# Softplus and split ahead of the weight conversion in each slot, and the sums of weight blocks on VectorE instead of GpSimd, in a decayed attention plus softplus FFN kernel

## The chip, the cores and the metric

The kernel runs on one core of a Trainium2 chip. The metric is the device time of one execution in microseconds (us); three timed runs before the change gave 600.14, 600.64 and 601.68 us, median 600.64. A core has five engines that each work through their own list of instructions in order and wait for each other by semaphores: TensorE (PE, with its weight loads shown as PEld), VectorE (DVE), ScalarE (ACT), GpSimd (POOL) and SyncE (SP, which issues most DMAs).

## What is computed

A causal attention without softmax, with a decay per head, over 4 sequences, 8 heads, 768 positions and 64 channels; its output, as 3072 tokens of width 512, goes through a feed-forward layer of width 2048 with a softplus between its two products.

```
for b in range(nb):
    intra = einsum('bhic,bhjc->bhij', qb, kb) * Dmask[None]
    intra = einsum('bhij,bhjd->bhid', intra, vb)
    inter = einsum('bhid,bhde->bhie', qb * lam_pow[None], kv_state)
    out[:, :, sl] = intra + inter
    kv_state = lam_block * kv_state + einsum('bhsd,bhse->bhde', kb_dec, vb)
h = x @ w_in
g = maximum(h, 0.0) + log1p(exp(-abs(h)))
return g @ w_out
```

## The kernel before

Tokens are worked on in six chunks of 512 (`NCH`), the feed-forward width in 16 blocks of 128 (`NF`). Each 32-bit product is made of three matmuls on operands split into a high and a low part: ACT writes the high part (a cast), DVE the low part (a subtraction from the high one). So what PE consumes always comes from an ACT step followed by a DVE step.

Every order is written out by hand: each engine runs its instructions in the order in which the program's lines emit them.

**Chunks 0 and 1.** The loop over `s` from 4 to 31 (line 657) is made of slots. Slot s holds the first product of chunk s // 16 with block s % 16 (`mlp1`, L421, 12 matmuls into a bank `h`) and, some slots later, the second product for an earlier slot (`mlp2`, L442, 12 matmuls). In between stand the softplus of the slot before (`chain_act`, ACT L402, from bank `h` to `l`), its split (`chain_hi`, ACT L406, and `chain_lo`, DVE L410, into tile `g`), and in slots 4 to 15 the conversion of the weights, which arrive as raw 64-bit numbers. A group of two weight blocks, tile `c`, is begun in one slot by ACT (`w_scale` L217, `w_round` L221) and DVE (`w_shift` L225, `w_sign` L229, `w_add` L235), and finished in the next slot by ACT (`w_hi` L238) and DVE (`w_lo` L242), which write tile `w`. In an even slot, the group that is finished there is the one that this slot's `mlp1` reads.

Attention comes in units of one pair of heads and one chunk. In slots 6, 9, 12 and 15 `scores_of` puts the score products on PE and, behind `w_add`, the masking (L338) and four state updates (L343) on DVE. In slots 5, 8, 11 and 14 the unit's output product `z` (L326 and L330) follows, with `x_high` (ACT L375) and `x_low` (DVE L393). From slot 16 on, every even slot runs `event`, which does the output of one unit and the scores of the next; its first instructions on PE are the `z` products of unit 8, which need the state updates of slot 15. `k_decay` (ACT L289, tile `kd`) and `q_decay` (DVE L296, `qd`) stand at the top of the slot before a unit's scores; in slot 15 they belong to unit 9, whose input `att` is loaded by SP (L86) into a buffer that the `z` products of slot 14 set free.

**Sums of weight blocks.** Chunks 2 to 5 need fewer first products, at the price of sums of weight blocks: seven products `P1` to `P7` (L588) on combinations of blocks. `block_sums(i)` (L514) forms the sums for one pair of weight blocks in tiles `full` and `sums` on POOL: two additions of 512 columns and four of 256. `store_sums` (L528) splits them (ACT L531, DVE L532) into a tile `parts`, and `send_sums` sends that to DRAM, from where `load_w1` fetches it later. All this is done in slots 16 to 31, one pair per two slots.

**Chunk 2's entry.** In slots 29 to 31 and right behind them the combinations of x are formed: `x_sums_early` and `x_sums_late` (DVE L568 to L577) and `x_block` (ACT L560, DVE L561, tiles `xcP1` to `xcP7`). Then the loop over i from 0 to 7 (line 735) runs, for each pair of weight blocks, P1 into bank `a`, P6 into `b`, P5 into `c`, then P2, P7, P4, P3. ACT copies `a` to `p1` (L753) behind P1, and P2, which adds to the same bank, has to wait for this copy.

```
        old, new = w_group(s - 1), w_group(s)
        if old:
            w_hi(*old)
        chain_act(s - 1)
        chain_hi(s - 1)
        if old:
            w_lo(*old)
        chain_lo(s - 1)
```

## Time and profile before

| what | before |
|---|---|
| median of three runs | 600.64 us |
| the profiled execution, its own time | 599.66 us |
| its span, first to last instruction | 597.7 us |
| PE busy | 578.1 us, 97% of the span |
| DVE busy | 309.6 us, 52% |
| ACT busy | 256.6 us, 43% |
| POOL busy | 53.3 us, 9% |
| L518, additions of 512 columns on POOL | 16, mean 1461 ns |
| L523 to L526, of 256 columns on POOL | 32, means 790 to 858 ns |

The profile's page gives busy times by engine and by 40 slices, the chain of work that ended last, and the costliest groups of instructions. The answers of the trace used below are: busy time in chosen stretches (windows), who waited for whom (waits), and the instructions in order of time (timeline). A row of the timeline has the start, the length, the engine, the line, the operation, what is written and read, the count, and in brackets how long the engine sat idle before it and what ended that. A busy PE is not PE at its peak, since matmuls are pipelined and their ends are modelled. PE is busy nearly all the time, so what counts is where it isn't.

### The profile page before, as it was taken

How to read it: one execution, taken by the hardware profiler on the slowest of the kernel's cores; microseconds unless marked ns; L12 is line 12 of the kernel's file. 1: busy time of each engine (PE TensorE's matmuls, PEld its weight loads, DVE VectorE, ACT ScalarE, POOL GpSimd, SP SyncE). 2: the span in 40 equal slices, each digit the busy share in tenths (PEclk: the TensorE clock that was granted, in tenths of full speed). 3: DMA queues.
4: the chain of work that ended last, by engine and by line, in shares of the span. 5: the costliest groups of instructions: out<-in, count | busy, mean ns of one | idle time of the engine just before them, and what ended most of it. 6: DMA issues, size and time to landing. Idle time of an engine off the chain costs nothing.

```text
span 597.7 us, 12023 instructions
## 1 busy us (share of the span) xinstructions
PE 578.1 (97%) x5203; PEld 471.9 (79%) x5203; DVE 309.6 (52%) x444; ACT 256.6 (43%) x416; POOL 53.3 (9%) x59
## 2 busy tenths in 40 slices
PE   8899898979999999999999999999999999999997
PEld 6676776758888888888888888888888888888886
DVE  7778988886556537735433443285133333333410
ACT  3776677653444436453432423463142222224310
POOL 2000000063533440000000000000000000000000
PEclk9999899998999999999999999999999999999999
DMA  8996546884599996889635556489357453474101
GB/s 293 406 407 252 178 153 197 276 268 165 186 389 393 408 416 256 328 312 394 226 135 194 198 207 234 173 296 362 133 212 316 145 196 136 145 268 141 62 1 70
DMA packets 38452, 142.34 MB, mean 238 GB/s; under 512 B 3712, under 2 KB 5760, under 8 KB 31360
## 3 DMA queue, kind: packets, MB, share of 16 engines
q1 hardware_dynamic: 35808, 136.86, 62.7%
q10 hardware_dynamic: 2592, 4.72, 2.1%
q8 instruction: 41, 0.67, 0.4%
q14 instruction: 11, 0.09, 0.0%
HBM read 112.20 MB, written 29.36 MB: 237 GB/s over the span
## 4 chain that ended last, share of the span: by engine, by line
PE 81%; DMA 11%; DVE 5%; ACT 1%; issue 1%; SPq 1%; DVEq 0%
PE o L607 31%; PE b L588 11%; PE h L421 9%; PE o L442 9%; PE a L588 7%; PE c L588 7%; DMA raw<-in_wts 6%; DMA g<-w 2%; PE z L326 2%; DMA att<-in_att 2%; PE x L311 2%; PE z L330 1%; DVE c L229 1%; DVE c L235 1%; DVE st L343 1%
## 5 line engine op out<-in xcount | busy, mean ns | idle before, releaser
L607 PE MATMUL o<-w,g 128*128 128x512 f32 x816 | 192.7, 390 | 0.0
L607 PEld LDWEIGHTS o<-w,g 128*128 128x128 f32 x816 | 152.5, 188 | 31.9
L421 PE MATMUL h<-x,w 128*128 128x512 f32 x384 | 96.0, 400 | 3.1 <-DVE w L242 2.8
L421 PEld LDWEIGHTS h<-x,w 128*128 128x128 f32 x384 | 72.1, 191 | 21.5 <-DVE w L242 4.5
L442 PE MATMUL o<-w,g 128*128 128x512 f32 x336 | 82.4, 394 | 1.1 <-DVE w L242 0.8
L442 PEld LDWEIGHTS o<-w,g 128*128 128x128 f32 x336 | 62.4, 188 | 15.2 <-DVE w L242 1.1
L588 PE MATMUL a<-xcP,w1a 128*128 128x512 f32 x192 | 48.8, 389 | 0.0
L588 PE MATMUL b<-xcP,w1b 128*128 128x512 f32 x192 | 48.7, 389 | 0.0
L755 DVE TENSOR_TENSOR ta<-b,ta 128x512 f32<-128x512 f32 x16 | 11.1, 691 | 62.9 <-PE b L588 62.9
L588 PEld LDWEIGHTS a<-xcP,w1a 128*128 128x128 f32 x192 | 36.0, 188 | 7.6
L588 PEld LDWEIGHTS b<-xcP,w1b 128*128 128x128 f32 x192 | 36.0, 188 | 7.5
L410 DVE TENSOR_TENSOR g<-l,g 128x512 fp32r<-128x512 f32 x32 | 24.8, 774 | 28.6 <-ACT g L406 28.6
L599 DVE TENSOR_TENSOR g<-lb,g 128x512 fp32r<-128x512 f32 x32 | 21.1, 688 | 34.1 <-ACT g L595 34.1
L763 DVE TENSOR_TENSOR tb<-b,ta 128x512 f32<-128x512 f32 x16 | 11.1, 691 | 52.7 <-PE b L588 52.7
L402 ACT ACTIVATE l<-h 128x512 f32<-128x512 f32 x32 | 19.0, 594 | 35.2 <-PE h L421 32.2
L518 POOL TENSOR_TENSOR full<-w 128x512 f32<-128x512 f32 x16 | 23.0, 1461 | 123.0 <-PE o L442 122.6
L760 ACT ACTIVATE la<-a 128x512 f32<-128x512 f32 x16 | 9.6, 598 | 54.6 <-PE a L588 54.6
L338 DVE TENSOR_TENSOR a<-x,mask 128x512 f32<-128x512 f32 x15 | 10.4, 692 | 41.4 <-PE x L311 21.5
L753 ACT COPY ta<-a 128x512 f32<-128x512 f32 x16 | 9.4, 586 | 52.1 <-PE a L588 52.1
L238 ACT CAST w<-c 128x1024 fp32r<-128x1024 f32 (+1 forms) x19 | 17.4, 913 | 29.2 <-DVE c L235 29.2
L326 PEld LDWEIGHTS z<-qd,st 64*64 64x64 f32 x640 | 17.6, 138 | 11.6 <-issue 11.2
L595 ACT CAST g<-lb 128x512 fp32r<-128x512 f32 x32 | 18.8, 619 | 18.4 <-PE o L607 17.6
(100 smaller groups left out, 803.4 us busy)
## 6 DMA issues: line engine op xcount, KB each, us to landing
w<-g SPq DMA_DIRECT2D x39, 1024.0 KB, 5.0
att<-in_att SPq DMA_DIRECT2D x48, 512.0 KB, 8.6
raw<-in_wts SPq DMA_DIRECT2D x32, 512.0 KB, 10.2
w1a<-g SPq DMA_DIRECT2D x16, 1024.0 KB, 6.4
g<-w SPq DMA_DIRECT2D x24, 512.0 KB, 8.8
w1b<-g SPq DMA_DIRECT2D x16, 768.0 KB, 6.2
g<-parts SPq DMA_DIRECT2D x16, 512.0 KB, 10.3
out_dram<-ob ACTq DMA_DIRECT2D x18, 256.0 KB, 2.2
```

Of the source, the lines that this page charges most:

```text
L238: nc.scalar.copy(out=w_at(ks)[:, 0], in_=conv[ks[0]].bitcast(F32))
L311: nc.tensor.matmul(x[r, cols], lhsT=k[r, b, t], rhs=q[r, b, t], start=True, stop=True)
L326: nc.tensor.matmul(w[half(t), s, cols], lhsT=st[r, b, t], rhs=qd[r, b, t], start=True, stop=False)
L402: nc.scalar.activation(l_tiles[s], h_tiles.pop(s), AF.Softplus)
L410: nc.vector.tensor_sub(out=g[:, 1, :], in0=l_tiles.pop(s), in1=g[:, 0, :])
L421: nc.tensor.matmul(h_tiles[s], lhsT=w[:, i, cs], rhs=x[:, j, :], start=p == 0 and n == 0, stop=p == NP - 1 and n == 2,)
L442: nc.tensor.matmul(o_tiles[c][b], lhsT=g[:, i, b * 128 : (b + 1) * 128], rhs=w[:, j], start=f == 0 and n == 0, stop=f == NF - 1 and n == 2,)
L518: nc.gpsimd.tensor_add(out=full[:, n], in0=w[:, 0], in1=w[:, 1])
L588: nc.tensor.matmul(to, lhsT=w[:, k, n, p * 128 : (p + 1) * 128], rhs=x[:, j, p], start=start and p == 0 and m == 0, stop=p == 1 and m == 2 ...
L595: nc.scalar.copy(out=g[:, 0], in_=l)
L599: nc.vector.tensor_sub(out=g[:, 1], in0=l, in1=g[:, 0])
L607: nc.tensor.matmul(outs[c, b], lhsT=g[:, i, b * 128 : (b + 1) * 128], rhs=w[:, j], start=f == 0 and n == 0, stop=f == NF - 1 and n == 2,)
```

## The change

Two things change. In each slot of chunks 0 and 1, the softplus of the slot before and both halves of its split are emitted ahead of the finishing of the weights; and the finishing's DVE half (`w_lo`) stays ahead of the new group's DVE steps, but behind `w_scale` and `w_round` in the program's text, which are on ACT. Second, the sums of weight blocks go from POOL to DVE. They are formed two slots later (pair 0 in slot 18 instead of 16, and so on), stored two slots later and sent two slots later, and the last pair is formed, stored and sent at the beginning of i = 1 of chunk 2's loop.

```diff
-            nc.gpsimd.tensor_add(out=full[:, n], in0=w[:, 0], in1=w[:, 1])
+            nc.vector.tensor_add(out=full[:, n], in0=w[:, 0], in1=w[:, 1])
...
-        nc.gpsimd.tensor_add(out=s1, in0=a21, in1=a22)
-        nc.gpsimd.tensor_sub(out=s3, in0=a11, in1=a21)
-        nc.gpsimd.tensor_sub(out=s2, in0=s1, in1=a11)
-        nc.gpsimd.tensor_sub(out=s4, in0=a12, in1=s2)
+        nc.vector.tensor_add(out=s1, in0=a21, in1=a22)
+        nc.vector.tensor_sub(out=s3, in0=a11, in1=a21)
+        nc.vector.tensor_sub(out=s2, in0=s1, in1=a11)
+        nc.vector.tensor_sub(out=s4, in0=a12, in1=s2)
...
+        chain_act(s - 1)
+        chain_hi(s - 1)
+        chain_lo(s - 1)
         old, new = w_group(s - 1), w_group(s)
         if old:
             w_hi(*old)
-        chain_act(s - 1)
-        chain_hi(s - 1)
-        if old:
-            w_lo(*old)
-        chain_lo(s - 1)
         if new:
             w_scale(*new)
             w_round(*new)
+        if old:
+            w_lo(*old)
...
-        if s > NF + 1 and s % 2 == 0:
-            send_sums((s - NF) // 2 - 1)
+        if s > NF + 2 and s % 2 == 0:
+            send_sums((s - NF) // 2 - 2)
...
-        if s >= NF and s % 2 == 0:
-            block_sums((s - NF) // 2)
-        if s >= NF and s % 2:
-            store_sums((s - NF) // 2)
+        if s > NF and s % 2 == 0:
+            block_sums((s - NF) // 2 - 1)
+        if s > NF + 2 and s % 2:
+            store_sums((s - NF - 1) // 2 - 1)
...
-    send_sums(NF // 2 - 1)
     chain_act(last - 1)
     chain_hi(last - 1)
     chain_lo(last - 1)
+    send_sums(NF // 2 - 2)
     x_sums_late(2, 1)
...
         for i in range(NF // 2):
+            if more and i == 1:
+                block_sums(NF // 2 - 1)
+                store_sums(NF // 2 - 1)
+                send_sums(NF // 2 - 1)
```

On ACT, at the top of slot 10, before the change (`c18` is the weight group that is finished, `c20` the one that is begun, `h9` the first product of slot 9):

```order
L238 CAST w9_1068<-c18_992 128x1024
L402 ACTIVATE l9_1070<-h9_1050 128x512
L406 CAST g9_1072<-l9_1070 128x512
L217 ACTIVATE c20_1076<-raw20_897 128x1024
L221 ACTIVATE raw20_897<-raw20_897 128x1024
```

And with the change:

```order
L402 ACTIVATE l9_1068<-h9_1050 128x512
L406 CAST g9_1070<-l9_1068 128x512
L238 CAST w9_1073<-c18_991 128x1024
L217 ACTIVATE c20_1075<-raw20_897 128x1024
L221 ACTIVATE raw20_897<-raw20_897 128x1024
```

The softplus and the split of `h9` now stand ahead of the cast of the weights, and `w_scale` directly behind that cast. On DVE, in slots 8 and 9, before the change:

```order
L235 ISA c16_913<-raw16_770,c16_913 128x2048
L393 TENSOR_TENSOR x_1_0_754<-z5_931,x_1_0_754 128x2x4x64
L242 TENSOR_TENSOR w8_984<-c16_913,w8_984 128x1024
L410 TENSOR_TENSOR g8_988<-l8_986,g8_988 128x512
L225 TENSOR_SCALAR c18_992<-c18_992 128x1024
```

And with the change:

```order
L235 ISA c16_912<-raw16_770,c16_912 128x2048
L393 TENSOR_TENSOR x_1_0_754<-z5_931,x_1_0_754 128x2x4x64
L410 TENSOR_TENSOR g8_986<-l8_984,g8_986 128x512
L242 TENSOR_TENSOR w8_989<-c16_912,w8_989 128x1024
L225 TENSOR_SCALAR c18_991<-c18_991 128x1024
```

The low part of the split (L410) and the finishing of the weights (L242) have changed places. On DVE at the beginning of i = 1 of chunk 2's loop (`g2_1` is the split of i = 0, `b2_1` the bank of P6), before the change:

```order
L599 TENSOR_TENSOR g2_1_2959<-tb2_0_2901,g2_1_2959 128x512
L296 TENSOR_TENSOR qd_18_3087<-att18_2787,lp_127 128x512
L755 TENSOR_TENSOR ta2_1_3089<-b2_1_3092,ta2_1_3089 128x512
```

And with the change:

```order
L599 TENSOR_TENSOR g2_1_2946<-tb2_0_2888,g2_1_2946 128x512
L518 TENSOR_TENSOR full7_3062<-w13_1338 128x512 x2
L523 TENSOR_TENSOR sums7_3065<-full7_3062 128x256
L524 TENSOR_TENSOR sums7_3065<-full7_3062 128x256
L525 TENSOR_TENSOR sums7_3065<-sums7_3065,full7_3062 128x256
L526 TENSOR_TENSOR sums7_3065<-full7_3062,sums7_3065 128x256
L532 TENSOR_TENSOR parts7_3070<-sums7_3065,parts7_3070 128x1024
L296 TENSOR_TENSOR qd_18_3087<-att18_2774,lp_127 128x512
L759 TENSOR_TENSOR ta2_1_3089<-b2_1_3092,ta2_1_3089 128x512
```

Seven DVE instructions of pair 7 now stand between the split of i = 0 and the first steps of i = 1; the matching ACT cast (L531) stands ahead of `kd` and of the copy of bank `a` in ACT's list. In slot 30 the same six instructions, L518 to L526, for pair 6, stand on DVE between the state updates and `x_sums_late`.

## The prediction

> **What bounds the kernel now.** PE is busy 97% of the span, so I first looked for where it is not: windows by stage, then PE's own waits there.

> ```profile
> 54.00:140.00 86.00, 76.40 (x846) 61.10 (x845) 75.49 (x90) 56.45 (x75) 11.49 (x8) 0.96 0.68 224
> 140.00:240.00 100.00, 100.00 (x1267) 82.76 (x1266) 57.69 (x84) 44.39 (x75) 37.69 (x40) 1.00 0.82 312
> PE z L326 <- DVE st L343: 4.5, 1, 4.5
> PE h L421 <- DVE w L242: 2.8, 2, 2.0
> PE w L311 <- DVE x L393: 2.0, 1, 2.0
> ```

> A windows row gives stretch, length, then busy time of PE, PEld, DVE, ACT and POOL, PE's granted clock, DMA share and GB/s. From 140 us (slot 16) on PE has no gap: nothing that shortens DVE there shortens the kernel, and a late result costs its whole lateness. From 54 to 140 us (slots 5 to 15) DVE is busy 75.5 of 86 us and every PE wait ends on DVE: the weight conversion on DVE paces these slots. So I followed DVE's and ACT's timeline there. One slot (8, then the top of 9):

> ```profile
> 75.90 1.23 DVE L242 TENSOR_TENSOR w<-c,w 128x1024 fp32r<-128x1024 f32 x1 [0.52 <-ACT w L238]
> 77.04 0.69 DVE L410 TENSOR_TENSOR g<-l,g 128x512 fp32r<-128x512 f32 x1
> 78.08 0.69 DVE L225 TENSOR_SCALAR c<-c 128x1024 uint32<-128x1024 uint32 x1 [0.34 <-ACT c L217]
> 78.81 1.23 DVE L229 SCALAR_TENSOR_TENSOR c<-raw,c 128x1024 uint32<-128x1024 uint32 x1
> 80.17 1.22 DVE L235 CUSTOM_DVE_ANT_0 c<-raw,c 128x2048 uint16<-128x2048 uint16 x1
> 74.81 1.05 ACT L238 CAST w<-c 128x1024 fp32r<-128x1024 f32 x1 [2.40 <-DVE c L235]
> 75.77 0.59 ACT L402 ACTIVATE l<-h 128x512 f32<-128x512 f32 x1
> 76.92 1.13 ACT L217 ACTIVATE c<-raw 128x1024 f32<-128x1024 f32 x1
> 81.43 1.05 ACT L238 CAST w<-c 128x1024 fp32r<-128x1024 f32 x1 [1.88 <-DVE c L235]
> ```

> The slot takes 6.62 us from cast to cast (74.81 to 81.43). DVE idles twice: 0.52 for the cast, and 0.34 because `w_scale` comes behind softplus and split.

> **Slots 4 to 14 with the change.** Distances between starts, from these rows: cast to L242 1.09; L242 to the next 1.14; L225 to L229 0.73; L229 to L235 1.36; L235 to the next cast 1.26. With L410 in the gap under the cast, and `w_scale` right behind the cast, L225 follows L242 at once: 1.09 + 1.14 + 0.73 + 1.36 + 1.26 = 5.58 us for a plain slot, instead of 6.62. Two things lengthen this.

> ```profile
> 87.93 0.68 DVE L338 TENSOR_TENSOR a<-w,mask 128x512 f32<-128x512 f32 x1
> 88.63 1.79 DVE L343 SCALAR_TENSOR_TENSOR st<-st,lam_c,w 64x256 f32<-64x256 f32 x4
> 90.45 1.23 DVE L242 TENSOR_TENSOR w<-c,w 128x1024 fp32r<-128x1024 f32 x1
> 91.73 2.79 PE L421 MATMUL h<-x,w 128*128 128x512 f32 x11 [2.05 <-DVE w L242]
> 48.53 1.23 DVE L242 TENSOR_TENSOR w<-c,w 128x1024 fp32r<-128x1024 f32 x1 [1.11 <-ACT w L238]
> 103.27 1.23 DVE L242 TENSOR_TENSOR w<-c,w 128x1024 fp32r<-128x1024 f32 x1 [0.52 <-ACT w L238]
> 117.40 1.23 DVE L242 TENSOR_TENSOR w<-c,w 128x1024 fp32r<-128x1024 f32 x1 [0.51 <-ACT w L238]
> ```

> First, behind slots 6, 9 and 12 stand mask and states (0.70 and 1.82 us), and L410, 0.60, is not hidden: L242 to L242 is 1.14 + 0.73 + 1.36 + 1.14 + 0.70 + 1.82 + 0.60 = 7.49. Second, the new wait: the cast queues behind a softplus that waits for PE. In an even slot where PE waits for L242 the loop is 1.28 to the products (90.45 to 91.73), 2.79 for eleven of them, 1.15 for softplus and split (75.77 to 76.92), 1.09 to the next L242: 6.3. Queued behind this ACT wait are cast, `w_scale`, and with them DVE.

> L242 stands at 48.53 in slot 4, 90.45 in slot 10, 103.27 in slot 12 and 117.40 in slot 14. From slot to slot, 4 to 14, I get 5.58, 5.58, 7.49, 5.58, 6.3, 7.49, 6.3, 6.5, 7.49, 5.58 (6.5, because the pair from 10 to 12 took 12.82 before with PE full, which the change doesn't alter), together 63.9 instead of 68.9. So L242 of slot 14 comes 5.0 us earlier and that of slot 12 about 3.9. PE runs full from there to the `z` of slot 14, so `z` moves by something between; I take 4.4.

> **Slot 15 and the restart of PE.**

> ```profile
> 117.36 0.80 SPq L86 DMA_DIRECT2D att<-in_att x2
> 123.29 0.91 ACT L289 ACTIVATE kd<-att,rp 128x256 f32<-128x256 f32 x2 [2.22 <-DMA att<-in_att]
> 125.17 1.54 DVE L242 TENSOR_TENSOR w<-c,w 128x1024 fp32r<-128x1024 f32 x1 [1.06 <-ACT w L238]
> 126.63 1.79 DVE L410 TENSOR_TENSOR g<-l,g 128x512 fp32r<-128x512 f32 x1
> 128.35 1.23 DVE L225 TENSOR_SCALAR c<-c 128x1024 uint32<-128x1024 uint32 x1
> 129.61 1.64 DVE L229 SCALAR_TENSOR_TENSOR c<-raw,c 128x1024 uint32<-128x1024 uint32 x1
> 131.38 1.53 DVE L235 CUSTOM_DVE_ANT_0 c<-raw,c 128x2048 uint16<-128x2048 uint16 x1
> 124.35 3.53 POOL L518 TENSOR_TENSOR full<-w 128x512 f32<-128x512 f32 x2 [112.37 <-PE o L442]
> 135.48 0.49 PE L326 MATMUL z<-qd,st 64*64 64x64 f32 x8 [4.51 <-DVE st L343]
> ```

> `kd` waits for unit 9, loaded once `z` of slot 14 is through (SP issues the load at 117.36); it moves with `z`, to 118.9 (a load 1.5 us quicker or slower moves the result as much). Then 0.82 for `kd`, 1.15 for softplus and split, now ahead, 1.09: L242 starts at 121.95, 3.2 earlier. In this slot POOL runs the first sums, and five DVE instructions take 1.54, 1.79, 1.23, 1.64 and 1.53 instead of 1.23, 0.69, 0.69, 1.23 and 1.22: 2.7 us. With POOL silent and L410 ahead, L242 to the end of the states is 1.14 + 0.73 + 1.36 + 1.14 + 0.70 + 1.82 = 6.9, so `z` of unit 8 starts near 129.0 instead of 135.48: **6.5 us gained**.

> PE then still waits: it was through at 130.97, 13.7 us behind `z` of slot 14, of which 0.8 was a wait for L242; so now at about 125.9, and waits 3.1 us instead of 4.5.

> ```profile
> 130.00:140.00 10.00, 5.49 (x139) 4.73 (x138) 8.64 (x12) 4.07 (x7) 5.91 (x5) 0.83 0.99 321
> ```

> Behind the long wait PE's clock is low: 0.83 over 10 us is at most 1.7 us lost, some of it in the wait itself. I take the same loss again. [...]

> **The sums on DVE.** DVE has 57.7 busy of 100 us between 140 and 240; six additions per two slots fit, with matmuls above them. No row has a 128x256 addition on DVE: half of the 0.69 of a 128x512 one is the lower bound, a quarter of the four state updates' 1.79 the upper. So a pair costs 2 x 0.69 + 4 x 0.35 = 2.8 to 3.2 us; I take 2.8, the row of the same operation being the nearer. Where DVE is tight it shows:

> ```profile
> 233.65 0.69 DVE L575 TENSOR_TENSOR tt<-xr,tt 128x512 f32<-128x512 f32 x1
> 245.19 1.89 DVE L561 TENSOR_TENSOR xcP<-tt,xcP 128x512 fp32r<-128x512 f32 x3
> 246.13 1.52 PE L588 MATMUL b<-xcP,w1a 128*128 128x512 f32 x6
> 247.16 0.57 ACT L753 COPY ta<-a 128x512 f32<-128x512 f32 x1
> 248.85 1.52 PE L588 MATMUL a<-xcP,w1a 128*128 128x512 f32 x6
> 261.80 0.69 DVE L599 TENSOR_TENSOR g<-tb,g 128x512 fp32r<-128x512 f32 x1
> 264.03 0.57 ACT L753 COPY ta<-a 128x512 f32<-128x512 f32 x1
> 266.09 1.52 PE L588 MATMUL a<-xcP,w1a 128*128 128x512 f32 x6
> 280.78 0.59 ACT L753 COPY ta<-a 128x512 f32<-128x512 f32 x1 [1.94 <-PE a L588]
> ```

> Pair 6 now stands ahead of L575 in slot 30. DVE and ACT have about 0.4 us of slack between there and the low part for P6, which so ends at 245.9 + 2.4 = 248.3. PE's sixth matmul of P6 wants it at 246.13 + 5 x 0.23 = 247.3: 1.0 us; then the copy of `a`, 2.4 later, ends at 250.1, while P2 would start at 248.85 + 1.0: 0.3 more. Pair 7 starts behind L599, at 262.4, and is through at 265.2; ACT's cast of 1.05 (as the 1.05 of L238, same size), `kd` 0.82 and the copy 0.57 end at 267.6, P2 wants it at 266.1: 1.5. These are **2.8 us given back**. The send of pair 7 also holds SP's queue until about 267, ahead of unit 19 and the weights of i = 2; P1 of i = 2 is copied only at 280.78, 14 us after that, so I count nothing, with 1.5 us if those loads come late.

> **The sum.** 599.66 (the execution, 1.96 more than its span) - 6.5 + 2.8 = 596.0. The median of the runs is 0.98 above that execution, so I predict 597.0.

> **Rivals.**
> - *The entry of chunk 2 costs nothing*, because DVE's additions are quicker or slack is larger: 600.64 - 6.5 = 594.1. For it: only 1.0, 0.3 and 1.5 us of lateness in long chains. 15%.
> - *No low clock behind the shorter wait*: 1.3 us more gained (of the 1.7 above), 595.7. For it: the wait of 2.05 at 91.73 is followed by eleven products in 2.79, full speed. Against it: 3.1 is nearer to 4.5. 15%. [...]
> - *Only POOL's part is gained.* If PE or the loads pace slots 4 to 14, as they did from 10 to 12, 2.7 + 0.6 for L410 - 2.8 = 0.5 is left: 600.1. 15%.
> - *ACT's queue turns into the pace.* If `h` is ready more than 1.15 us behind the add in every slot, softplus and split are exposed each time: 5.58 + 1.15 = 6.73 in seven slots and 7.49 + 1.15 = 8.64 in three, 73.0 instead of 68.9, so 4.1 later; slot 15 gives back 2.1 (3.3 less 1.15), the entry costs 2.8: 605.4. Against it: in slot 10 `h` ends at 91.73 + 2.79 = 94.5, and the add, by the distances above, at 90.45 + 1.14 + 0.60 + 0.73 + 1.36 + 1.22 = 95.5. 5%. [...]
> - *The change doesn't do what it says*: its order on ACT and DVE shows that it does; no chance.

> **Chances.** My forecast 50%, 595.5 to 598.5 by itself. Over 0.3% (1.8 us, about what a measurement of this kernel can tell from no change) faster, under 598.84: the forecast's 50 less 4 for its tail, the first two rivals' 30, in all 76%; within 0.3%: the third rival and that tail, 19%; slower 5%. The range leaves out the slow rival and the tails: 594.0 to 600.2.

> **What would show it.** L242's distances 5.6 in plain slots and 6.3 behind an even one; five DVE durations back at 1.23, 0.69, 0.69, 1.23, 1.22 in slot 15; the `z` of unit 8 near 129.0 with a wait of about 3.1 and a low clock behind; new PE waits of 1.0 and 0.3 at chunk 2's P6 and P2 and of 1.5 at P2 of i = 1. Wrong would be: slots that stay at 6.6, a load of unit 9 that no longer follows `z`, or PE without those last waits.

## The result, and the profile after

The changed kernel takes 595.83 us (median of four runs, 595.38 to 596.39) against 600.76 for the kernel before (median of four). The ratio is 0.9917, 95% interval 0.9900 to 0.9934: 4.9 us faster. From profiled execution to profiled execution the difference is 3.8 us (599.66 to 595.9), in the span 3.6 us (597.7 to 594.1).

Windows by stage after the change, in the columns used in the prediction:

```profile
54.00:140.00 86.00, 80.91 (x893) 64.79 (x885) 73.75 (x93) 56.53 (x75) 0.00 (x0) 1.00 0.70 230
140.00:240.00 100.00, 99.98 (x1267) 82.60 (x1265) 70.46 (x124) 44.14 (x76) 0.00 (x0) 1.00 0.81 305
```

Who waited for whom on PE, after (total, times, longest):

```profile
PE z L326 <- DVE st L343: 2.9, 1, 2.9
...
PE a L588 <- ACT ta L757: 1.5, 1, 1.5
...
PE b L588 <- DVE xcP L561: 0.4, 1, 0.4
PE b L588 <- ACT xcP L560: 0.4, 1, 0.4
```

In the stretch from 54 to 140 us PE is busy 80.91 us instead of 76.40, at a clock of 1.00 instead of 0.96. The wait of 2.0 us for L393 is gone, the wait for the states is 2.9 instead of 4.5. Three waits on L588, the products of chunk 2, are new. DVE has 12.8 us more to do between 140 and 240 (70.46 for 57.69), and POOL nothing.

The timeline of DVE and ACT after, from L242 of slot 7 over a plain slot and an even one behind it:

```profile
67.72 1.22 DVE L242 TENSOR_TENSOR w<-c,w 128x1024 fp32r<-128x1024 f32 x1
...
72.68 0.68 DVE L410 TENSOR_TENSOR g<-l,g 128x512 fp32r<-128x512 f32 x1
73.28 1.22 DVE L242 TENSOR_TENSOR w<-c,w 128x1024 fp32r<-128x1024 f32 x1
...
77.38 0.60 ACT L402 ACTIVATE l<-h 128x512 f32<-128x512 f32 x1 [1.57 <-PE h L421]
...
79.62 1.22 DVE L242 TENSOR_TENSOR w<-c,w 128x1024 fp32r<-128x1024 f32 x1 [0.26 <-ACT w L238]
```

The plain slot takes 73.28 - 67.72 = 5.56 us; the even one, in which ACT's softplus waits 1.57 us for PE, 79.62 - 73.28 = 6.34. In the same view, slot 15 on DVE, ACT and PE:

```profile
113.27 1.22 DVE L242 TENSOR_TENSOR w<-c,w 128x1024 fp32r<-128x1024 f32 x1
...
119.77 0.91 ACT L289 ACTIVATE kd<-att,rp 128x256 f32<-128x256 f32 x2 [3.95 <-DMA att<-in_att]
...
121.84 0.69 DVE L410 TENSOR_TENSOR g<-l,g 128x512 fp32r<-128x512 f32 x1 [2.92 <-ACT g L406]
122.79 1.23 DVE L242 TENSOR_TENSOR w<-c,w 128x1024 fp32r<-128x1024 f32 x1 [0.26 <-ACT w L238]
123.94 0.69 DVE L225 TENSOR_SCALAR c<-c 128x1024 uint32<-128x1024 uint32 x1
124.66 1.23 DVE L229 SCALAR_TENSOR_TENSOR c<-raw,c 128x1024 uint32<-128x1024 uint32 x1
126.02 1.22 DVE L235 CUSTOM_DVE_ANT_0 c<-raw,c 128x2048 uint16<-128x2048 uint16 x1
...
129.81 0.34 PE L326 MATMUL z<-qd,st 64*64 64x64 f32 x8 [2.94 <-DVE st L343]
```

The first row is L242 of slot 14. The five instructions are back at 0.69, 1.23, 0.69, 1.23 and 1.22, and `z` of unit 8 stands at 129.81 instead of 135.48: 5.67 us earlier. Its matmuls take 0.34 instead of 0.49, since the clock did not fall behind the wait (1.00, where it was 0.50 before). The `mlp2` behind it (L442) is 6.89 earlier; its rows before and after the change:

```profile
138.73 1.65 PE L442 MATMUL o<-w,g 128*128 128x512 f32 x6
131.84 3.03 PE L442 MATMUL o<-w,g 128*128 128x512 f32 x12
```

From `z` to this `mlp2` it took 3.25 us before, at the low clock (0.50 from 134.80 to 138.21 us), and takes 2.03 now, at 1.00.

In the same view, the entry of chunk 2. The first row is P1 of i = 0 before the change, the others are after it: P1, DVE with pair 6 in slot 30, PE in P6 and at P2, then ACT with pair 7 and PE at P2 of i = 1:

```profile
244.77 1.52 PE L588 MATMUL a<-xcP,w1a 128*128 128x512 f32 x6
...
237.78 1.52 PE L588 MATMUL a<-xcP,w1a 128*128 128x512 f32 x6
...
226.70 1.29 DVE L518 TENSOR_TENSOR full<-w 128x512 f32<-128x512 f32 x2
228.02 0.43 DVE L523 TENSOR_TENSOR sums<-full 128x256 f32<-128x256 f32 x1
...
229.50 0.68 DVE L575 TENSOR_TENSOR tt<-xr,tt 128x512 f32<-128x512 f32 x1
...
240.36 0.73 PE L588 MATMUL b<-xcP,w1a 128*128 128x512 f32 x2 [0.38 <-ACT xcP L560]
241.51 0.50 PE L588 MATMUL b<-xcP,w1a 128*128 128x512 f32 x1 [0.42 <-DVE xcP L561]
...
243.37 1.67 PE L588 MATMUL a<-xcP,w1a 128*128 128x512 f32 x6
...
260.07 1.05 ACT L531 CAST parts<-sums 128x1024 fp32r<-128x1024 f32 x1 [2.58 <-DVE sums L526]
...
262.45 1.65 PE L588 MATMUL a<-xcP,w1a 128*128 128x512 f32 x6 [1.51 <-ACT ta L757]
```

A pair costs 229.50 - 226.70 = 2.80 us of DVE. The lead of PE over the profile of before is 244.77 - 237.78 = 6.99 us at P1, 248.85 - 243.37 = 5.48 at P2, 266.09 - 262.45 = 3.64 at P2 of i = 1: 3.35 us are given back here. The three waits shown make up 2.3 of that; the rest probably goes where PE stops and starts between single matmuls (one alone takes 0.50, six in a row 1.52).

### The profile page after: what moved, and what is told of

Same layout as the page of the kernel before. It is cut to its first block, busy times and chain, and to the rows that moved or that the text cites. A ratio compares the mean times of both kernels' runs of the same rounds, so it can differ in the third digit from the quotient of the medians.

```text
span 594.1 us, 12014 instructions
## 1 busy us (share of the span) xinstructions
PE 576.5 (97%) x5203; PEld 469.4 (79%) x5203; DVE 321.6 (54%) x492; ACT 256.8 (43%) x416; POOL 4.1 (1%) x11
## 4 chain that ended last, share of the span: by engine, by line
PE 76%; DVE 10%; DMA 8%; ACT 2%; issue 1%; SPq 1%; DVEq 0%; ACTq 0%
PE o L607 30%; PE b L588 11%; PE h L421 8%; PE o L442 8%; PE c L588 7%; PE a L588 7%; DMA att<-in_att 4%; DMA g<-w 3%; PE x L311 2%; PE z L326 2%; DVE c L235 2%; DVE st L343 2%; DMA raw<-in_wts 1%; DVE w L242 1%; DVE c L229 1%
## 5 line engine op out<-in xcount | busy, mean ns | idle before, releaser
L421 PE MATMUL h<-x,w 128*128 128x512 f32 x384 | 94.4, 395 | 2.1 <-DVE w L242 2.1
L421 PEld LDWEIGHTS h<-x,w 128*128 128x128 f32 x384 | 70.9, 188 | 19.9 <-DVE w L242 3.7
L442 PE MATMUL o<-w,g 128*128 128x512 f32 x336 | 82.3, 393 | 1.1 <-DVE w L242 0.8
L442 PEld LDWEIGHTS o<-w,g 128*128 128x128 f32 x336 | 62.3, 188 | 15.1 <-DVE w L242 1.2
L588 PE MATMUL a<-xcP,w1a 128*128 128x512 f32 x192 | 49.0, 391 | 1.5 <-ACT ta L757 1.5
L588 PE MATMUL b<-xcP,w1b 128*128 128x512 f32 x192 | 48.8, 389 | 0.0
L588 PEld LDWEIGHTS a<-xcP,w1a 128*128 128x128 f32 x192 | 35.9, 188 | 9.8 <-ACT ta L757 2.3
L588 PEld LDWEIGHTS b<-xcP,w1b 128*128 128x128 f32 x192 | 36.0, 188 | 7.5
L402 ACT ACTIVATE l<-h 128x512 f32<-128x512 f32 x32 | 19.0, 595 | 49.1 <-PE h L421 46.5
L599 DVE TENSOR_TENSOR g<-lb,g 128x512 fp32r<-128x512 f32 x32 | 21.1, 688 | 34.1 <-ACT g L595 34.1
L338 DVE TENSOR_TENSOR a<-x,mask 128x512 f32<-128x512 f32 x15 | 10.4, 691 | 44.1 <-PE y L313 23.4
L410 DVE TENSOR_TENSOR g<-l,g 128x512 fp32r<-128x512 f32 x32 | 22.1, 690 | 18.8 <-ACT g L406 18.7
L588 PE MATMUL b<-xcP,w1a 128*128 128x512 f32 x96 | 24.9, 391 | 0.8 <-DVE xcP L561 0.4
L326 PEld LDWEIGHTS z<-qd,st 64*64 64x64 f32 x640 | 17.0, 134 | 10.0 <-issue 9.7
L386 ACT COPY xr<-z 128x512 f32<-128x512 f32 x16 | 9.4, 585 | 36.0 <-PE z L330 35.5
```

Of the source, the lines that this page charges most:

```text
L326: nc.tensor.matmul(w[half(t), s, cols], lhsT=st[r, b, t], rhs=qd[r, b, t], start=True, stop=False)
L402: nc.scalar.activation(l_tiles[s], h_tiles.pop(s), AF.Softplus)
L410: nc.vector.tensor_sub(out=g[:, 1, :], in0=l_tiles.pop(s), in1=g[:, 0, :])
L421: nc.tensor.matmul(h_tiles[s], lhsT=w[:, i, cs], rhs=x[:, j, :], start=p == 0 and n == 0, stop=p == NP - 1 and n == 2,)
L442: nc.tensor.matmul(o_tiles[c][b], lhsT=g[:, i, b * 128 : (b + 1) * 128], rhs=w[:, j], start=f == 0 and n == 0, stop=f == NF - 1 and n == 2,)
L588: nc.tensor.matmul(to, lhsT=w[:, k, n, p * 128 : (p + 1) * 128], rhs=x[:, j, p], start=start and p == 0 and m == 0, stop=p == 1 and m == 2 ...
```

## The experiments

Each kernel ran beside the kernel before on the same chip: E1 to E4 together (before: 600.87 us, 17 runs), E5 to E8 (600.43, 11 runs), E9 to E11 (599.99, 13 runs), E12 (600.4, 15 runs). The theory going in: of the 5.7 us at `z` of unit 8, 3.0 come from the order and 2.7 from a silent POOL; the sums on DVE give 3.4 back at the entry of chunk 2.

**E1, the order alone.** The sums go back to POOL and to their old slots (two of the places, against the changed kernel):

```diff
-            nc.vector.tensor_add(out=full[:, n], in0=w[:, 0], in1=w[:, 1])
+            nc.gpsimd.tensor_add(out=full[:, n], in0=w[:, 0], in1=w[:, 1])
...
-            block_sums((s - NF) // 2 - 1)
+            block_sums((s - NF) // 2)
...
```

> The kernel before with only the new order within the slots; the sums stay on GpSimd in their old slots. My theory (of the 5.7 us that z of unit 8 came earlier, 2.7 are from a silent GpSimd and 3.0 from the order; 3.4 us are given back by the sums on VectorE): z of unit 8 near 132.5 instead of 135.5, slots 5 to 14 at the distances of after (5.58, 6.34, 7.5), no new wait at the entry of chunk 2, the wait of 4.5 us before z of unit 8 still there with its low clock: about 3 us below before, near 597.7. Rival (the order alone pays nothing, since PE or the loads pace these slots, and the gain is that of the silent GpSimd): within 0.5 us of before, 600.3.

Measured: 595.05 us, ratio 0.9917 (0.9904 to 0.9930), as much as the whole change. The rival fell, and of the theory the size (597.7 was expected). The timeline of slot 15 in E1, on POOL, DVE and PE:

```profile
120.20 2.53 POOL L518 TENSOR_TENSOR full<-w 128x512 f32<-128x512 f32 x2 [108.22 <-PE o L442]
...
122.06 1.22 DVE L410 TENSOR_TENSOR g<-l,g 128x512 fp32r<-128x512 f32 x1 [3.13 <-ACT g L406]
...
125.06 1.65 DVE L229 SCALAR_TENSOR_TENSOR c<-raw,c 128x1024 uint32<-128x1024 uint32 x1
126.84 1.54 DVE L235 CUSTOM_DVE_ANT_0 c<-raw,c 128x2048 uint16<-128x2048 uint16 x1
...
130.95 0.49 PE L326 MATMUL z<-qd,st 64*64 64x64 f32 x8 [3.67 <-DVE st L343]
```

POOL's first additions now fall into the 3.13 us in which DVE waits for unit 9 anyway, so its instructions are stretched by 0.53 + 0.42 + 0.32 = 1.3 us, not 2.7. `z` comes 4.53 us earlier by the order alone, and PE has no wait at the entry of chunk 2.

**E2, the sums alone**: the changed kernel with the slot order of before.

```diff
-        chain_act(s - 1)
-        chain_hi(s - 1)
-        chain_lo(s - 1)
         old, new = w_group(s - 1), w_group(s)
         if old:
             w_hi(*old)
+        chain_act(s - 1)
+        chain_hi(s - 1)
+        if old:
+            w_lo(*old)
+        chain_lo(s - 1)
...
-        if old:
-            w_lo(*old)
```

> The kernel after with the order of before within the slots: only the sums moved, to VectorE and one or two slots later. My theory: the five VectorE instructions of slot 15 go back to 1.23, 0.69, 0.69, 1.23, 1.22, z of unit 8 comes 2.7 us earlier (132.8), the slots stay at 6.6, and the entry of chunk 2 gives 3.4 back: 0.7 us slower than before, 601.4, the same within what can be measured. Rival (the sums are where the whole gain comes from): as after, 596.

Measured: 599.58 us, ratio 1.0004 (0.9983 to 1.0025): no change, as expected. `z` of unit 8 stands at 133.23, 2.25 earlier; PE waits at the entry of chunk 2 as in the changed kernel (1.5 before P2 of i = 1, 0.4 and 0.3 in P6). The twelve runs fall into two groups: eight from 598.85 to 600.9, and four from 603.05 to 604.39 with a mean clock of 0.985 to 0.988, of which none was profiled. So the two parts, 4.53 and 2.25 alone, make 5.67 together: beside the new order a silent POOL is worth 1.14.

**E3, the sums in their new slots, but on POOL**, all five lines of the kind:

```diff
-            nc.vector.tensor_add(out=full[:, n], in0=w[:, 0], in1=w[:, 1])
+            nc.gpsimd.tensor_add(out=full[:, n], in0=w[:, 0], in1=w[:, 1])
```

> The kernel after, with the sums in their new slots but formed on GpSimd again. My theory: nothing of the sums runs in slot 15 or 16's tight part, so z of unit 8 stays near 129.8, and VectorE has 2.8 us less to do in slot 30 and at i = 1 of chunk 2, but two-input VectorE instructions beside the GpSimd additions are stretched by about 1 to 2 us there: half to all of the 3.4 us of the entry come back, 592.5 to 594.5. Rival (the entry is late because pair 7's cast on ScalarE waits for the sums, which take GpSimd longer): as after or slower, 596 to 598, with the copy of bank a at i = 1 later than 261.8.

Measured: 594.63 us, ratio 0.9901 (0.9886 to 0.9916). That is 0.1 above the range expected. The three waits of PE at the entry are gone; one of 0.77 us is new. The timeline there, DVE and PE:

```profile
239.02 4.09 DVE L561 TENSOR_TENSOR xcP<-tt,xcP 128x512 fp32r<-128x512 f32 x3
...
244.98 1.66 PE L588 MATMUL b<-xcP,w1b 128*128 128x512 f32 x6 [0.77 <-DVE ta L759]
```

Three subtractions beside POOL's additions take 4.09 us; three of the same take 1.89 at 229.33 in the same run. So POOL costs DVE 2.2 us there, of which PE sees the 0.77. In the profiled run the clock was low (0.50) from 129.62 to 133.03 us, behind the 2.89 us wait before `z` of unit 8.

**E4, `x_sums_late(2, 0)` ahead of pair 6's sums in slot 30.**

```diff
+        if s == last - 2:
+            x_sums_late(2, 0)
         if s > NF and s % 2 == 0:
             block_sums((s - NF) // 2 - 1)
...
         if s == last - 2:
-            x_sums_late(2, 0)
```

> The kernel after, with the late half of x_sums of chunk 2 ahead of pair 6's sums in slot 30; nothing else moves. Theory A (VectorE's stretch from 226.7 to 243.8 has no gap, so the 2.8 us of work delay P6 wherever they stand in it): as after within 0.5 us, 595.8, with the same waits of PE in P6. Theory B (it is the place ahead of the late half that delays P6): 1.5 us faster, 594.3, and those waits of PE gone.

Measured: 597.0 us, ratio 0.9941 (0.9928 to 0.9954). It is not quicker, and P6 still waits 0.59 and 0.42 us (0.38 and 0.42 in the changed kernel): theory B fell. Where the work stands in DVE's full stretch makes no gain. Theory A's time, 595.8, was met by the profiled run (595.75) and missed by 1.2 us in the median, which these traces don't explain.

**E5, pair 7 behind the addition that forms `u2` of i = 1 (DVE, bank `b` of P6 plus `p1`). E6, pair 6 to the same place of i = 0.** The expectations call this addition the low part for u2. E5, then E6:

```diff
-            if more and i == 1:
-                block_sums(NF // 2 - 1)
-                store_sums(NF // 2 - 1)
-                send_sums(NF // 2 - 1)
...
+            if more and i == 1:
+                block_sums(NF // 2 - 1)
...
+            if more and i == 1:
+                store_sums(NF // 2 - 1)
+                send_sums(NF // 2 - 1)
```

```diff
-        if s > NF and s % 2 == 0:
+        if s > NF and s % 2 == 0 and s < last - 2:
             block_sums((s - NF) // 2 - 1)
...
+            if more and i == 0:
+                block_sums(NF // 2 - 2)
...
```

> The kernel after, with the sums of pair 7 moved behind the low part for u2 of i = 1, and their store and send behind the second split of i = 1. My theory (ScalarE's cast for pair 7 stands ahead of the copy of bank a and waits for the sums, so P2 of i = 1 starts 1.5 us late): that wait of PE goes and nothing replaces it, 1.5 to 1.8 us below after, near 594.2. Rival (VectorE is full there too, so the work delays the next split instead, or the blocks are sent too late for what reads them): as after, 595.8, with a new wait of PE within the next 15 us.

> The kernel after, with the sums of pair 6 moved out of slot 30 to i = 0 of chunk 2, behind the low part for u2. My theory (VectorE's full stretch into P6 is 2.8 us longer for them): PE's waits of 0.7 to 0.9 us in P6 and those before P2 go, 1.5 us below after, near 594.3. Rival (the work then delays the split of i = 0, since pair 7 follows it closely): half or less of it, 595 to 596, with a longer wait before P2 of i = 1.

Measured: 595.59 (0.9914, 0.9899 to 0.9929) and 595.39 (0.9914, 0.9897 to 0.9932). The waits went where they should: E5 has none before P2 of i = 1, E6 none in P6, and nothing took their place. The medians are only 0.2 and 0.4 us below the changed kernel's, and the runs differ in the granted clock: at a mean clock of 0.999 or more the span is 593.6 to 594.1 us in the changed kernel (three runs), 592.4 in E5 and 592.1 in E6 (one run each), at least 1.2 and 1.5 less. But two such runs of E4 differ by 1.0 us (593.9 and 594.9), so this is weak evidence. In time these two are not settled; E8 is.

**E7, the decays of unit 9 in slot 15 behind the conversion.**

```diff
-        if s + 1 in units_at:
+        if s + 1 in units_at and s != NF - 1:
...
+        if s == NF - 1:
+            k_decay(units_at[s + 1])
+            q_decay(units_at[s + 1])
```

> The kernel after, with the decays of unit 9 in slot 15 moved behind the steps of the conversion, so that ScalarE's softplus and cast no longer queue behind the load of unit 9. My theory (this load, which follows z of slot 14, holds back softplus, cast and with it everything up to the states of unit 8): the cast near 117.6 instead of 121.7, the wait of 2.9 us before z of unit 8 gone, 2.5 to 3 us below after, near 593. Rival (the decays are then late for the scores of unit 9, or weights not yet loaded hold the cast): as after, 595.8, with a wait of 2 to 3 us elsewhere in slot 15 or 16.

Measured: 593.29 us (592.94 to 593.4), ratio 0.9879 (0.9865 to 0.9893). The timeline of slot 15 in E7, on ACT, DVE and PE:

```profile
117.38 0.60 ACT L402 ACTIVATE l<-h 128x512 f32<-128x512 f32 x1 [1.56 <-PE h L421]
...
118.54 1.05 ACT L238 CAST w<-c 128x1024 fp32r<-128x1024 f32 x1
...
121.62 0.89 ACT L289 ACTIVATE kd<-att,rp 128x256 f32<-128x256 f32 x2
...
127.24 0.34 PE L326 MATMUL z<-qd,st 64*64 64x64 f32 x8 [0.42 <-DVE st L343]
```

The cast comes 3.2 us earlier (0.9 later than expected, since the softplus ahead of it waits for PE), `z` of unit 8 2.57 us earlier, and `kd` at 121.62 waits for nothing. The load of unit 9 was what held slot 15 back.

**E8, E5 to E7 together.**

> The three moves together: pairs 6 and 7 behind the low parts for u2 of i = 0 and i = 1, and the decays of unit 9 in slot 15 behind the conversion. If the three waits are independent, the gains add up: 1.5 + 1.6 + 2.8, about 590. If VectorE has no room for two pairs so close to each other, one of the first two is lost: 591.5 to 593.

Measured: 589.45 us (589.17 to 589.92), ratio 0.9817 (0.9803 to 0.9831), faster than both kernels. Its windows by stage:

```profile
54.00:140.00 86.00, 83.43 (x888) 66.84 (x888) 74.14 (x93) 57.65 (x77) 0.00 (x0) 1.00 0.69 230
140.00:240.00 100.00, 100.00 (x1268) 83.14 (x1268) 71.73 (x126) 45.52 (x79) 0.00 (x0) 1.00 0.86 324
```

PE is busy 83.43 us in the first stretch and without a gap in the second; no wait on L588 is left. From E7 to E8 are 593.29 - 589.45 = 3.84 us: the entry's whole price, 3.35 by the trace, is won back by the place of pairs 6 and 7 alone.

**E9, the low part of the split behind the finishing of the weights again,** and **E10, cast and scaling ahead of softplus and split.** E9, then E10:

```diff
-        chain_lo(s - 1)
         old, new = w_group(s - 1), w_group(s)
...
         if old:
             w_lo(*old)
+        chain_lo(s - 1)
```

```diff
-        chain_act(s - 1)
-        chain_hi(s - 1)
-        chain_lo(s - 1)
         old, new = w_group(s - 1), w_group(s)
...
             w_round(*new)
+        chain_act(s - 1)
+        chain_hi(s - 1)
+        chain_lo(s - 1)
```

> The kernel after, but the low part of the split on VectorE stands behind the finishing of the weights again; softplus and split on ScalarE stay ahead of the cast, the scaling directly behind it. My theory (the low part fills the 1.09 us that VectorE waits for the cast): plain slots of 6.2 instead of 5.58, mask slots unchanged at 7.5, z of unit 8 about 2 us later than in after (131.8), 597.5 to 598. Rival (the scaling directly behind the cast is all that matters): distances of 5.58 as in after, 595.8.

> The kernel after, but ScalarE casts and scales the weights ahead of softplus and split, and the low part of the split on VectorE stands ahead of the finishing of the weights still, so VectorE waits for the split there. My theory (VectorE's wait before the finishing then lasts from cast to the end of the split, 1.05 + 2.2 + 1.2 + 0.5 = about 5 us of ScalarE in each slot): slots of 7.5 or more, z of unit 8 some 10 us later than in after, 605 or more. Rival (only VectorE's order counts): as after.

Measured: E9 599.28 us (0.9983, 0.9971 to 0.9995), `z` of unit 8 at 132.65; E10 627.04 us (1.0450, 1.0432 to 1.0468), `z` of unit 8 at 160.81. DVE's timeline of E9, two rows of L242:

```profile
55.60 1.23 DVE L242 TENSOR_TENSOR w<-c,w 128x1024 fp32r<-128x1024 f32 x1 [0.52 <-ACT w L238]
...
61.77 1.23 DVE L242 TENSOR_TENSOR w<-c,w 128x1024 fp32r<-128x1024 f32 x1 [0.51 <-ACT w L238]
```

And of E10, two rows of L242 with what stands ahead of the second, then `z` of unit 8 on PE:

```profile
79.96 1.22 DVE L242 TENSOR_TENSOR w<-c,w 128x1024 fp32r<-128x1024 f32 x1
...
88.56 0.69 DVE L410 TENSOR_TENSOR g<-l,g 128x512 fp32r<-128x512 f32 x1 [3.65 <-ACT g L406]
89.17 1.22 DVE L242 TENSOR_TENSOR w<-c,w 128x1024 fp32r<-128x1024 f32 x1
...
160.81 0.34 PE L326 MATMUL z<-qd,st 64*64 64x64 f32 x8 [0.99 <-DVE st L343]
```

In E9 a plain slot takes 6.17 us, and the gap of 0.52 under the cast is back, as expected: L410 in that gap is worth 0.6 a slot. `z` is 2.84 us later than with the change, not 2, and the median is 1.3 above the range expected. In E10 a slot takes 9.21 us: DVE waits 3.65 us for the split, which queues behind cast and scaling on ACT. So within this order it is the softplus and the split ahead of the cast that make the rest possible. The direction was expected, its size was far too low: `z` of unit 8 comes 31.0 us later than with the change, where some 10 were expected, and the run takes 31.2 us more.

**E11, E7's move with the order alone**, the sums on POOL in their old slots.

> The order of after and the decays of unit 9 in slot 15 behind the conversion, with the sums left on GpSimd in the slots of before: no sums on VectorE, no cost at the entry of chunk 2. My theory: GpSimd's additions stretch VectorE's instructions of slot 15 by 1.3 us or more again, z of unit 8 near 128.5 with a wait of PE of 1.7 us and full clock: about 1.3 us above the version with all three moves, 590.5 to 591.5. Rival (GpSimd's additions run where VectorE has its gaps): as the version with all three moves, 589.5.

Measured: 594.84 us, ratio 0.9908 (0.9891 to 0.9924), no better than E1; both expectations fell. The timeline of slot 15 in E11, on DVE and PE:

```profile
121.20 1.79 DVE L225 TENSOR_SCALAR c<-c 128x1024 uint32<-128x1024 uint32 x1
123.03 2.20 DVE L229 SCALAR_TENSOR_TENSOR c<-raw,c 128x1024 uint32<-128x1024 uint32 x1
125.37 1.54 DVE L235 CUSTOM_DVE_ANT_0 c<-raw,c 128x2048 uint16<-128x2048 uint16 x1
126.83 1.22 DVE L296 TENSOR_TENSOR qd<-att,lp 128x512 f32<-128x512 f32 x1
...
130.62 0.45 PE L326 MATMUL z<-qd,st 64*64 64x64 f32 x8 [3.35 <-DVE st L343]
```

With the load's wait gone, POOL's additions meet a busy DVE: 1.10 + 0.97 + 0.32 + 0.53 = 2.9 us of stretch, a wait of 3.35 and a low clock (0.50 to 0.68 from 130 to 134 us). What E7 wins on DVE, POOL takes. So what the sums' move is worth in slot 15 depends on whether something else makes DVE wait there.

**E12, the order alone, with 14 matmuls in the wait of PE.**

```diff
+        x, y = (bank(f"x{g}"), bank(f"y{g}")) if g < NG else (None, None)
+        if g == 2 * NP + 1:
+            for _ in range(14):
+                nc.tensor.matmul(x, lhsT=warm[:, :128], rhs=warm, start=True, stop=True)
         mm_out(g - 1, w)
         if g < NG:
-            x, y = bank(f"x{g}"), bank(f"y{g}")
```

> The kernel with only the new order (sums on GpSimd in their old slots), plus 14 matmuls of 128x512 on a bank that is free, in TensorE's list right ahead of z of unit 8, where TensorE waits 3.67 us for the states; at the full clock they take 3.2 us, and their results are overwritten. Clock theory (the wait is what brings the clock down to half for the 6 to 8 us behind it): the granted clock stays at 1.00 through 130 to 140 us, the mean clock of every run is 0.998 or more instead of 0.994 to 0.997, z of unit 8 starts at 130.95 as before, and the run is 1.5 to 3 us quicker than the order alone: 592 to 593.5. Rival (the low clock has another cause, or the matmuls hold z back by as much): 595, with a low clock in the same stretch.

Measured: 601.55 us, ratio 1.0014 (1.0004 to 1.0025). It doesn't answer the question. A load of weights is issued at 111.79 instead of 104.70 in E1, the finishing of slot 14 and all behind it are late, and PE waits 3.85 us ahead of the `mlp2` that stands before the 14 matmuls. Probably this is because they keep the tile `warm` in use for longer, so that the rotating buffers of the loads are shared out in another way; the edit also takes the banks `x` and `y` ahead of the `z` products. Neither was tried apart. No experiment prices the low clock by itself; what the traces show of it is the 1.22 us between `z` of unit 8 and the `mlp2` behind it (3.25 before, 2.03 with the change).

## Why the prediction was right, point by point

The predicted median was 597.0 us, the measured one is 595.83, inside the range; the profiled execution was put at 596.0 and took 595.9. Part of that is luck, since the terms were off by up to 1.2 us on either side.

- **Slots 4 to 14: right.** L242's distances are 5.58, 5.56, 7.50, 5.56, 6.34, 7.49, 6.34, 6.76, 7.50, 5.56, together 64.2 for 63.9. E9 and E10 show the two causes named, L410 under the cast and the ACT queue. L242 of slot 14 is 4.13 us earlier, not 5.0: 0.55 because slot 4 itself began later (49.08 for 48.53), which the prediction took as fixed. So `z` of slot 14 gained 3.35, not 4.4, and `kd` stood at 119.77 instead of 118.9. The order alone does not make that late start: in E3, with the same order, L242 of slot 4 stands at 48.42, and `z` of unit 8 at 129.09, where the prediction had 129.0.
- **Slot 15: right in kind, 0.8 too large.** `z` of unit 8 gained 5.67 instead of 6.5, the 0.9 of `kd` handed on. From L242 to `z` it takes 7.02 us for the 6.9 worked out. What the prediction took as POOL's share, 2.7, is its share with the order of before; E2 measures 2.25 there, and E1 and the change together 1.14. That shifts the credit, not the sum: the gain of the change is that of the order.
- **PE's wait: right; the low clock behind it: wrong.** The wait is 2.94 us (3.1 predicted) and the clock stays at 1.00; the matmuls behind lost nothing, 6.89 - 5.67 = 1.2 us more. The second rival, at 1.3, described this. The length of the wait alone does not decide it here: in E3 and E6 waits of 2.89 and 2.78 us were followed by a clock of 0.50 (the last section shows how these waits lie).
- **The entry of chunk 2: right in place, 0.6 too small.** A pair costs the 2.8 predicted. P6 and P2 lost 1.5 for 1.3, P2 of i = 1 some 1.8 for 1.5. E5, E6 and E8 show that these delays are the sums' and that they can be avoided; E4 that the place within slot 30 is not the cause. The loads behind pair 7's send were not late, as predicted.
- **The sum.** 599.66 - 5.67 - 1.22 + 3.35 = 596.1 for the 595.9 measured. The 0.98 added for the median was the mis-sized term of the last step: it stood for the scatter of the kernel before, of which the change has less. Of 17 runs of the kernel before beside E1, those with a mean clock of 0.993 or more have spans of 597.4 to 598.2, those with 0.991 or less 598.7 to 599.9. In the profile of before there are two stretches of low clock (0.50), behind the 2.0 us wait (63.1 to 66.5 us) and behind the 4.5 us one (134.8 to 138.2); in that of the change there is none until 592.9 us, its last microseconds.
- **The rivals.** That only POOL's part is gained was given 15%; E1 and E2 show the reverse. That ACT's queue becomes the pace did not happen: the softplus waits for PE in each of slots 7 to 14 (0.35 to 2.45 us), but only three distances, 6.34, 6.34 and 6.76, are longer for it, for the 6.3, 6.3 and 6.5 worked out. E10 is what it looks like when an ACT queue does set the pace.

So the sums' move was worth nothing that can be measured here: E1 without it and the changed kernel stand at the same ratio, 0.9917, to the kernel before. The move saves 1.14 us and the low clock at slot 15 and pays 3.35 at the entry of chunk 2. With two pairs put elsewhere and slot 15's load out of the way (E8) it pays: 589.45 against 594.84 for E11.

## What to carry to other kernels

- Where two engines hand a value back and forth, put the instruction whose input is ready into the gap in which the other engine works: one subtraction under a cast was worth 0.6 us in each plain slot, and with cast and scaling ahead of the softplus a slot took 9.21 us instead of 5.56.
- Work that is moved to another engine has to be priced at every place where that engine is full, and the stall that it removes is worth only what no other stall covers: gains measured alone (4.53 and 2.25) made 5.67 together.
- After a gain, look at what the engine now waits for first: here a load at the head of ACT's list, and moving the two decays behind the conversion brought 2.5 us.

## What the runs showed of the hardware

```profile
126.21:129.62 3.41, 0.53 (x34) 0.56 (x38) 3.31 (x8) 1.05 (x1) 2.53 (x2) 1.00 0.98 362
129.62:133.03 3.41, 3.41 (x110) 3.19 (x102) 1.79 (x3) 1.91 (x4) 2.08 (x3) 0.50 0.95 334
...
125.27:128.69 3.42, 1.60 (x7) 0.97 (x6) 3.25 (x5) 2.25 (x4) 0.00 (x0) 1.00 0.92 309
128.69:132.10 3.41, 2.29 (x129) 2.25 (x130) 2.92 (x6) 1.07 (x3) 0.00 (x0) 1.00 0.99 241
```

  In E3 nearly the whole wait lies in one step, in which PE is busy for only 0.53 us, and the next step has the low clock. In the changed kernel a wait as long is split over two steps, with PE busy for 1.60 and 2.29 us, and the clock stays. From the first change of each trace up to 560 us, all 11 steps at the full clock in which PE was busy for less than 0.93 us were followed by the low clock, and no step with more than 2.0 us was. Between 1.4 and 2.0 us five were and most were not; in four of the five only a wait of 1.4 to 2.0 us stands beside stretches of 64x64 matmuls (before, E6, E9, E11). What decides there is not shown. Part of the scatter goes with this: E3 to E6 and E9, with waits of 2.8 to 3.0 us, spread over 1.8 to 3.0 us (the changed kernel's four over 1.0), E7 and E8, which have no wait of that length, over 0.5 and 0.75. E2 does not fit: its wait is 2.32 us, and its runs spread over 5.5.
- **POOL beside DVE.** In slot 15 of before, E1 and E11 most of DVE's instructions on SBUF operands took longer beside additions on POOL, a one-input one too (L225: 0.69 to 1.79 in E11); two that began 0.22 and 0.58 us ahead of the addition beside them did not (L225 in E1, 0.68, and L242 at 120.06 in E11, 1.23). The mask and the state updates, which read a bank, keep their 0.68 and 1.79 in E1 and E11 beside POOL's additions. What holds DVE up there is not shown.
- **Small additions on DVE.** With the change a 128x256 addition (L523 to L526) takes 0.42 or 0.43 us, more than half of the 0.68 or 0.69 of a 128x512 one (L575), and starts 0.33 to 0.45 us behind the one before.
